# A convolution slot moved to the border between two products, and loads paced earlier, in a fused convolution and gated product

## The chip, the core and the metric

The kernel runs on one core of one Trainium2 chip. A core has engines that run beside each other: TensorE (matmuls, which write to PSUM), VectorE and ScalarE (which read PSUM and write SBUF), GpSimd and SyncE; the last two here mostly issue DMAs. In the profile they are PE (with PEld for the loading of weights), DVE, ACT, POOL and SP. The metric is the device time of one launch in microseconds (us). The kernel before takes 523.81 us, the median of three runs between 523.74 and 524.0.

## What is computed

The reference has two parts. The first is a causal convolution along the sequence, with 7 taps that each of 8 heads has for its 24 channels; the taps are a softmax of the weights. The second is a product of two projections, followed by two more products:

```python
# B, S, D = 8, 3904, 192; H, K = 8, 7; group = D // H = 24
w = softmax(weight)                                   # per head, over the 7 taps
out = np.einsum('hk,bskhg->bshg', w, x_unf)           # x_unf: x padded by 6 rows, windows of 7
x = out.reshape(B * S, D)                             # 31232 x 192
a = x @ w1                                            # 192 -> 1024
b = x @ w2
h = a * b @ w3                                        # 1024 -> 1024
return (h @ w_out).astype(np.float32)                 # 1024 -> 192
```

## The kernel before

**Tokens and rounds.** The 31232 tokens are cut in two streams of 15616 (`NS = 2`), which lie side by side: 64 of the 128 partitions belong to each. A round is 512 tokens of each stream (`CH`); there are 31 rounds (`NR`), the last of 256. Four rounds form a group (`GROUP`); there are eight groups, 0 to 7, the last of three rounds.

**First product** (`first_product`, L361, matmuls at L374). For a round and each of its eight feature tiles of 128 (0 to 7 in the text), twelve matmuls of 64 x 128 weights on 512 tokens make product a and product b of both streams. Each product fills one pair of PSUM banks. ScalarE copies a to SBUF (L380); VectorE multiplies the copy with b out of PSUM and writes the tile of `abT` (L381). Its input is `xT`, the transposed convolution, in three slices k of 128 channel rows, in a ring for four rounds (`RING`).

**Second product** (`second_product`, L388, matmuls at L400). `w3` and `w_out` are multiplied once at the start (`w3_product`, L433), so that one product from 1024 to 192 is left. For a round and one stream it takes 32 matmuls into one pair; ScalarE copies the result to `osb` (L405), and a DMA stores it (L412).

**PSUM pairs.** There are four pairs. `banks()` takes the first of a list of free ones and `drained()` puts a pair at the end of it, so all users take the pairs in rotation, in the order in which the program is written. A matmul that is to write a pair waits until the reader of its last content is done.

**Convolution** (`conv`, L262, matmuls at L278). The tokens are cut in 272 windows of 58 new tokens and 6 rows before them (64 rows). A head of a block of windows takes four 64 x 64 matmuls side by side with a banded matrix (`Aband`) as the weights' side and the block's x on the other. One head takes one pair, and VectorE (in group 0 partly ScalarE) moves it to `convo` (L295); heads 2 and 5 are moved in two pieces. Blocks 0 to 3 are small and belong to the prologue; blocks 4 to 9 have 36 windows, block 10 has 20. Block 4 is convolved in group 0 besides block 5, block 5 + p in group p.

**From the convolution back to the products.** When the last head of a block is moved, `store` (L300) writes it to DRAM (`rows`, L318 and L314), and `transposes` (L343, L347) reads it back transposed into `xT`, three DMAs to a round. Both are issued by SyncE's queue, which holds the output stores too and works strictly in order. `send(last)` (L479) issues the transposes of all rounds up to `last` whose rows are stored; after the first product of round R it is called with R + 4, since that product frees the ring for it. So a block's rows are normally needed a whole group after they are stored. The rows of block 4 are an exception: they feed rounds 4 to 7, which is group 1, right behind the group in which block 4 is convolved.

**Order of the work.** The program's order is written out by hand. In each group after the first come the first products of its rounds, then eight second products (two streams for each round, numbered 0 to 7), and between those the heads of one block, in three slots: `at` says after which second product which heads stand. The text calls the place where first products end and second products begin the border. Group 0's first products are in the prologue; its second products have six slots, three with block 4 and three with block 5.

**Loads of x.** GpSimd's queue issues them (`load_x`, L98, L112) in two halves of a block, one after each of the first two first products of the group that convolves it. What holds them back is a copy of two elements (`pace`, L528), which waits until a certain tile of `abT` is written. `zero` (L504, L506) then clears the padding rows of windows that begin a sequence.

Of the kernel before, what the change touches and what calls it, by code (L numbers as in the profile page):

```python
# [16 lines left out]
def kernel(  # L17
# [13 lines left out]
    H, K = weight.shape  # L31
    G = D // H
    DFF = moe_w1.shape[1]
    JT = DFF // 128
# [6 lines left out]
    GROUP = 4  # L41
# [9 lines left out]
    NB = len(SIZES)  # L51
# [4 lines left out]
    def tok(i):  # L56
        return (i // WB) * S + (i % WB) * ST
# [78 lines left out]
    pace = const.tile([1, 2], BF16)  # L136
# [31 lines left out]
    for p0 in (0, Q):  # L168
        nc.gpsimd.affine_select(
            out=diag[p0:p0 + Q], in_=ones[p0:p0 + Q].to_broadcast([Q, Q + PAD]),  # L170
# [3 lines left out]
    for r in range(NS):  # L174
        nc.gpsimd.dma_start(out=xb0[Q * r + PAD:Q * r + Q, 0, :],
                            in_=x_rows[r * TS:r * TS + ST, :])
# [13 lines left out]
    def warm(n, t=None):  # L190
# [16 lines left out]
        out=wall, in0=wall, in1=wmax.unsqueeze(2).to_broadcast([1, H, K]), op=ALU.subtract)  # L207
# [6 lines left out]
        out=wrow, in0=wall, in1=wsum.unsqueeze(2).to_broadcast([1, H, K]), op=ALU.mult)  # L214
# [47 lines left out]
    def conv(b, h0, nh, evict=None):  # L262
        n = SIZES[b] // 2
        if h0 == 0:
            convo_of[b] = work.tile([128, n, NP, NS, Q], BF16, tag="convo", bufs=2, name="convo")
        convo = convo_of[b]
        p, cps = banks()
        wd = nh * G

        def view(ps, r):  # L270
            return cps[ps, r, 0:n * wd].rearrange("p (w g) -> p w g", g=wd)

        for j in range(nh):
            h = h0 + j
            for c in range(2):
                xb, w0 = xb_of[b][c]
                for r in range(NS):
                    nc.tensor.matmul(  # L278
                        view(slice(Q * c, Q * c + Q), r)[:, :, j * G:(j + 1) * G],
                        band_of(h, r),  # L280
                        xb[Q * r:Q * r + Q, w0:w0 + n, h * G:(h + 1) * G],
                        start=True, stop=True)
        src = cps[:, :, 0:n * wd].rearrange("p r (w g) -> p r w g", g=wd)
        o, moves = 0, []
        for k, c0, m in segments(h0 * G, wd):
            moves.append((convo[:, :, k, :, c0:c0 + m].rearrange("p w r g -> p r w g"),
                          src[:, :, :, o:o + m]))
            o += m
        if h0 + nh == H:
            del xb_of[b]  # L290
        if evict == ():
            return p, moves
        for e, (dst, part) in enumerate(moves):
            f = evict or [nc.scalar.copy]
            f[e % len(f)](out=dst, in_=part)  # L295
        drained(p)
# [3 lines left out]
    def store(b, first=0, last=NWIN, queue=nc.sync):  # L300
        n = SIZES[b] // 2
        last = min(last, FIRST[b] + 2 * n)
        stored[0] = tok(last) if last < NWIN else TS
        convo = convo_of[b]
        for c in range(2):
            i0 = FIRST[b] + c * n
            w, end = max(0, first - i0), min(n, last - i0)
            while w < end:
                left = WB - 1 - (i0 + w) % WB
                m = min(end - w, max(1, left))  # L310
                src = convo[Q * c:Q * c + ST, w:w + m].rearrange("s w k r g -> s w (k r g)")
                j0 = tok(i0 + w)
                if left == 0:
                    queue.dma_start(out=rows[j0:j0 + LAST, :], in_=src[0:LAST, 0, :])  # L314
                else:
                    dst = rows[j0:j0 + ST * m, :].rearrange("(w s) c -> s w c", s=ST)
                    for s0, s1 in ((0, 48), (48, ST)):
                        queue.dma_start(out=dst[s0:s1], in_=src[s0:s1])  # L318
                w += m
# [36 lines left out]
    abT_of = {}  # L356
# [4 lines left out]
    def first_product(R, between=None):  # L361
        N = width(R)
        ab = work.tile([128, JT, NS, CH], BF16, tag="abT", bufs=GROUP, name="abT")
        abT_of[R] = ab
        r0 = (R * CH) % RING
        for ft in range(JT):
            pq = []
            for i in range(2):
                q, p = banks()
                pq.append((q, p))  # L370
                for k in range(NP):
                    for r in range(NS):
                        rs = slice(Q * r, Q * r + Q)
                        nc.tensor.matmul(  # L374
                            p[:, r, 0:N], wd[i][rs, k, ft * 128:(ft + 1) * 128],
                            xT[k][rs, r0:r0 + N],
                            start=(k == 0), stop=(k == NP - 1))
            (qa, pa), (qb, pb) = pq
            asb = work.tile([128, NS, CH], BF16, tag="asb", bufs=3, name="asb")
            nc.scalar.copy(out=asb[:, :, 0:N], in_=pa[:, :, 0:N])  # L380
            nc.vector.tensor_tensor(out=ab[:, ft, :, 0:N], in0=asb[:, :, 0:N],  # L381
                                    in1=pb[:, :, 0:N], op=ALU.mult)
            drained(qa)
            drained(qb)
            if between and ft in between:
                between[ft]()
# [55 lines left out]
    V, A, P = nc.vector.tensor_copy, nc.scalar.copy, nc.gpsimd.tensor_copy  # L442
# [33 lines left out]
    def need(R):  # L476
        return next(i for i in range(NWIN) if tok(i) >= (R + 1) * CH)

    def send(last):  # L479
        while sent[0] <= min(last, NR - 1) and min((sent[0] + 1) * CH, TS) <= stored[0]:  # L480
            transposes(sent[0])
            sent[0] += 1
# [21 lines left out]
    def zero(b):  # L504
        for xb, r, w in zero_rows.pop(b, []):
            nc.gpsimd.memset(xb[Q * r:Q * r + PAD, w, :], 0.0)  # L506

    def conv_heads(b, heads, f=(nc.vector.tensor_copy,), first=None):
        for j, h in enumerate(heads):
            conv(b, h, 1, (f[j % len(f)],))  # L510
        if heads[-1] == H - 1:
            store(b) if first is None else (store(b, last=first), send(NR), store(b, first))

    slots = (range(0, 3), range(3, 6), range(6, H))
    zero(4)
    for jt in range(JT):
        w3_product(jt)
# [3 lines left out]
    for p, rounds in enumerate(groups):  # L521
        b = PROLOGUE_BLOCKS + p
        order = rounds[-1:] + rounds[:-1] if rounds[-1] == NR - 1 else rounds
        for j, R in enumerate(order if p else ()):
            first_product(R)
            send(R + GROUP)
            if j < 2 and b < NB:
                P(out=pace, in_=abT_of[R][0:1, JT - 1, 1, 0:2])  # L528
                load_x(b, (j,))
        if b < NB:  # L530
            zero(b)
        at = {1: [(b, slots[0])], 3: [(b, slots[1])], 5: [(b, slots[2])]}
        if p == 0:
            at = {0: [(4, slots[0], (V, A))], 1: [(4, slots[1], (V, A))],
                  2: [(4, slots[2], (V, A), need(GROUP))], 4: at[1], 5: at[3], 6: at[5]}
        for i, (R, r) in enumerate((R, r) for R in rounds for r in range(NS)):
            second_product(R, r, R == NR - 1 and r == 1, nc.sync if p else nc.gpsimd)
            for c in at.get(i, ()) if b < NB else ():
                conv_heads(*c)
            if p == 0 and i == 2:  # L540
                send(2 * GROUP - 1)
# [31 lines left out]
```

## Time and profile before

| what | value |
|---|---|
| median of the runs | 523.81 us |
| time of the profiled execution | 523.65 us |
| its span, from first to last instruction | 521.9 us |
| TensorE busy in the span | 513.1 us (98%) |
| VectorE, ScalarE, GpSimd busy | 360.1, 322.3, 59.0 us |
| first products, L374 | 319.9 us busy, 2976 matmuls |
| second products, L400 | 166.1 us busy, 1952 matmuls |
| convolution, L278 | 16.6 us busy, 352 matmuls |
| granted clock of TensorE | 1.000 |

The profile follows one execution of the program. Its groups of instructions carry the line of the kernel, the engine, the operation and the names of the tiles. A chain of waits is followed back from the last instruction; an engine whose name stands on nearly all of the chain sets the time. Timelines give the start and the length of pieces of work in us from the start of the span, and in brackets the idle time before and what ended it. A matmul's recorded length covers its whole passage through the array, so matmuls overlap; what one costs is the distance from one start to the next. The time of a run is 1.75 us above the span of the profiled execution. The landing of SyncE's DMAs is not in the timelines, but the trace keeps every update of the semaphores that they raise.

### The profile page before, as it was taken

The page shows a single profiled execution, that of the slowest core. Times are in us where ns is not written, and L with a number is a line of the kernel's source. Part 1 is how long each engine was busy: PE and PEld are TensorE (multiplying, and loading weights), DVE is VectorE, ACT ScalarE, POOL GpSimd, SP SyncE. Part 2 cuts the span into 40 slices and gives each one's busy share as a digit, 9 for nine tenths or more (in the row PEclk, how much of TensorE's full clock was granted, in tenths as well). Part 3 has the DMA queues.
Part 4 walks back from the last instruction along what each step waited for, and adds up shares of the span by engine and source line. Part 5 has one row for each costly group of instructions (what it writes and reads, how often), then busy time and mean ns, then how long its engine had stood idle before and what let it go on. Part 6 is the DMA issues. An engine that isn't in the chain of part 4 may idle for free.

```text
span 521.9 us, 12776 instructions
## 1 busy us (share of the span) xinstructions
PE 513.1 (98%) x5452; PEld 340.3 (65%) x5452; DVE 360.1 (69%) x350; ACT 322.3 (62%) x405; POOL 59.0 (11%) x99
## 2 busy tenths in 40 slices
PE   8999899999999999999999999999999999999997
PEld 4544588545894558945588455884558855599667
DVE  6779646799537995389953899538994299912880
ACT  5877553777437774377743777437774377735762
POOL 8420522030000200003000020000200000000000
PEclk9999999999999999999999999999999999999999
DMA  9995998799656973569735696457724531024004
GB/s 127 206 155 104 141 197 253 168 188 158 142 152 162 114 104 92 156 164 124 92 98 154 159 125 88 107 150 163 99 49 120 154 97 33 17 92 152 3 1 152
DMA packets 135179, 65.39 MB, mean 125 GB/s; under 512 B 91980, under 2 KB 134318, under 8 KB 135058
## 3 DMA queue, kind: packets, MB, share of 16 engines
q1 hardware_dynamic: 95952, 44.45, 37.2%
q0 software_dynamic: 39024, 20.03, 29.3%
q8 instruction: 42, 0.69, 0.6%
q14 instruction: 15, 0.12, 0.1%
q10 hardware_dynamic: 146, 0.10, 0.1%
HBM read 33.25 MB, written 36.92 MB: 134 GB/s over the span
## 4 chain that ended last, share of the span: by engine, by line
PE 91%; DMA 3%; SPq 2%; ACT 2%; DVE 1%; issue 1%; POOL 0%; POOLq 0%; ACTq 0%
PE pairs L374 56%; PE pairs L400 31%; PE pairs L278 2%; DMA w3T<-w3rows 2%; SPq L430 2%; ACT asb L380 1%; DVE abT L381 1%; DMA xb<-in_x_dram 1%; PE pairs L436 0%; DVE convo L295 0%; PE pairs L327 0%; POOL xb L165 0%; DVE convo L445 0%; ACT xT L445 0%; SPq L347 0%
## 5 line engine op out<-in xcount | busy, mean ns | idle before, releaser
L381 DVE TENSOR_TENSOR abT<-asb,pairs 128x1024 bf16<-128x1024 bf16 (+1 forms) x248 | 298.4, 1204 | 74.2 <-ACT asb L380 37.1
L374 PE MATMUL pairs<-xT,wd 64*128 64x512 bf16 (+1 forms) x2976 | 319.9, 373 | 1.1 <-DVE convo L295 0.3
L380 ACT CAST asb<-pairs 128x1024 bf16<-128x1024 f32 (+1 forms) x248 | 247.6, 998 | 69.7 <-PE pairs L374 69.2
L374 PEld LDWEIGHTS <-wd 64*128 64x128 bf16 x2976 | 162.6, 94 | 152.9 <-issue 3.2
L400 PE MATMUL pairs<-W_sb,abT 128*128 128x192 bf16 x1952 | 166.1, 246 | 0.0
L400 PEld LDWEIGHTS <-abT 128*128 128x128 bf16 x1952 | 159.6, 98 | 9.7 <-issue 9.7
L405 ACT COPY osb<-pairs 128x384 f32<-128x384 f32 x122 | 58.2, 477 | 116.1 <-PE pairs L400 116.1
L295 DVE CAST convo<-pairs 128x864 bf16<-128x864 f32 (+6 forms) x71 | 53.0, 803 | 69.3 <-PE pairs L278 69.3
L112 POOL DMA_DIRECT2D xb<-in_x_dram x40 | 30.9, 790 | 9.0 <-issue 4.9
L528 POOL COPY pace<-abT 1x2 bf16<-1x2 bf16 x10 | 1.7, 174 | 238.7 <-DVE abT L381 238.7
L278 PE MATMUL pairs<-xb,Aband 64*64 64x432 bf16 (+3 forms) x352 | 16.6, 294 | 0.2 <-DMA xb<-in_x_dram 0.2
L278 PEld LDWEIGHTS <-Aband 64*64 64x64 bf16 x352 | 6.6, 105 | 7.1 <-issue 6.3
L412 POOL DMA_DIRECT2D out_dram<-osb x8 | 6.1, 760 | 18.5 <-ACT osb L405 18.5
L405 DVE COPY osb<-pairs 128x192 f32<-128x192 f32 x1 | 0.4, 358 | 11.1 <-PE pairs L400 11.1
L436 PE MATMUL pairs<-wo_b,w3T 128*128 128x192 bf16 x64 | 5.6, 246 | 1.9 <-DMA w3T<-w3rows 1.9
L436 PEld LDWEIGHTS <-w3T 128*128 128x128 bf16 x64 | 5.2, 98 | 2.5 <-DMA w3T<-w3rows 2.1
L295 ACT CAST convo<-pairs 128x512 bf16<-128x512 f32 (+4 forms) x11 | 6.2, 604 | 0.5 <-PE pairs L278 0.4
L438 ACT CAST W_sb<-pairs 128x192 bf16<-128x192 f32 x8 | 2.5, 318 | 4.8 <-PE pairs L436 4.8
L318 POOL DMA_DIRECT2D rows<-convo x6 | 3.5, 590 | 16.3 <-DVE convo L295 11.1
L195 PE MATMUL pairs<-zeros 128*128 128x512 bf16 x8 | 3.7, 595 | 1.3 <-DVE zeros L145 1.3
L327 PE MATMUL pairs<-identw,convo 128*128 128x128 bf16 x42 | 3.2, 219 | 1.0 <-DVE convo L445 0.6
L506 POOL MEMSET xb<- 6x192 bf16 x6 | 1.5, 249 | 21.4 <-DMA xb<-in_x_dram 21.4
(52 smaller groups left out, 42.5 us busy)
## 6 DMA issues: line engine op xcount, KB each, us to landing
out_dram<-osb SPq DMA_DIRECT2D x52, 384.0 KB
xb<-in_x_dram POOLq DMA_DIRECT2D x18, 432.0 KB, 7.3
rows<-convo SPq DMA_DIRECT2D x8, 648.0 KB
out_dram<-osb POOLq DMA_DIRECT2D x8, 384.0 KB, 5.0
w3rows<-in_moe_w_dram POOLq DMA_DIRECT2D x2, 1024.0 KB, 11.1
xb<-in_x_dram POOLq DMA_DIRECT2D x6, 240.0 KB, 6.7
xT<-rows SPq DMA_TRANSPOSE x84
rows<-convo SPq DMA_DIRECT2D x4, 324.0 KB
```

What stands on the lines that cost most here:

```text
L112: nc.gpsimd.dma_start(out=xb[Q * r:Q * r + Q, w:w + m, :], in_=x_spans(r, i, m))
L195: nc.tensor.matmul(t[:, j % 2, :], zeros[:, 0:128], zeros, start=True, stop=True)
L278: nc.tensor.matmul(view(slice(Q * c, Q * c + Q), r)[:, :, j * G:(j + 1) * G], band_of(h, r), xb[Q * r:Q * r + Q, w0:w0 + n, h * G:(h + 1) ...
L295: f[e % len(f)](out=dst, in_=part)
L374: nc.tensor.matmul(p[:, r, 0:N], wd[i][rs, k, ft * 128:(ft + 1) * 128], xT[k][rs, r0:r0 + N], start=(k == 0), stop=(k == NP - 1))
L380: nc.scalar.copy(out=asb[:, :, 0:N], in_=pa[:, :, 0:N])
L381: nc.vector.tensor_tensor(out=ab[:, ft, :, 0:N], in0=asb[:, :, 0:N], in1=pb[:, :, 0:N], op=ALU.mult)
L400: nc.tensor.matmul(ops[:, (g - g0) * D:(g - g0) * D + D], ab[:, jt, r, g * 128:(g + 1) * 128], W_sb[:, jt, :], start=(jt == 0), stop=(jt = ...
L405: f(out=osb[:, g0:g0 + per, :].rearrange("p g d -> p (g d)"), in_=ops[:, 0:per * D])
L412: queue.dma_start(out=out[t0:t0 + ng * 128, :].rearrange("(g p) d -> p g d", p=128), in_=osb)
L430: nc.sync.dma_start_transpose(out=w3T[:, gt, j:j + CH], in_=w3rows[j:j + CH, gt * 128:(gt + 1) * 128])
L436: nc.tensor.matmul(wps[:, 0, 0:D], w3T[:, gt, jt * 128:(jt + 1) * 128], wo_b[:, gt, :], start=(gt == 0), stop=(gt == JT - 1))
```

## The change

Two things are changed. First, the heads of a block are cut in slots of 2, 3 and 3 instead of 3, 3 and 2, and in groups 1 to 5 the first slot moves to the border, before the first second product; the other two stand after the second products 1 and 3. The slot after 5 is gone. In group 0 the slots stay where they are, with the new numbers of heads for block 4 and block 5. Second, the copy that paces the loads of x reads tile 3 of `abT` (the middle of a first product) instead of tile 7 (its end).

```diff
-    slots = (range(0, 3), range(3, 6), range(6, H))
+    slots = (range(0, 2), range(2, 5), range(5, H))
...
             if j < 2 and b < NB:
-                P(out=pace, in_=abT_of[R][0:1, JT - 1, 1, 0:2])
+                P(out=pace, in_=abT_of[R][0:1, JT // 2 - 1, 1, 0:2])
                 load_x(b, (j,))
         if b < NB:
             zero(b)
-        at = {1: [(b, slots[0])], 3: [(b, slots[1])], 5: [(b, slots[2])]}
+        at = {1: [(b, slots[1])], 3: [(b, slots[2])]}
         if p == 0:
             at = {0: [(4, slots[0], (V, A))], 1: [(4, slots[1], (V, A))],
-                  2: [(4, slots[2], (V, A), need(GROUP))], 4: at[1], 5: at[3], 6: at[5]}
+                  2: [(4, slots[2], (V, A), need(GROUP))],
+                  4: [(b, slots[0])], 5: [(b, slots[1])], 6: [(b, slots[2])]}
+        elif b < NB:
+            conv_heads(b, slots[0])
         for i, (R, r) in enumerate((R, r) for R in rounds for r in range(NS)):
             second_product(R, r, R == NR - 1 and r == 1, nc.sync if p else nc.gpsimd)
             for c in at.get(i, ()) if b < NB else ():
```

## The prediction

> **What bounds the kernel now.** I read the busy shares first, then the chain of waits in order of time, then single records at the places that the change touches, and the DMA queues there.
>
> ```profile
> span 521.9 us, 12776 instructions
> PE 513.1 (98%) x5452; PEld 340.3 (65%) x5452; DVE 360.1 (69%) x350; ACT 322.3 (62%) x405; POOL 59.0 (11%) x99
> ```
>
> TensorE is busy 98% of the span. The chain of waits in order of time, group 1 (rounds 4 to 7), shows how tight it is:
>
> ```profile
> 92.07 41.55 PE pairs L374 x384
> 133.62 5.39 PE pairs L400 x64
> 139.00 0.67 PE pairs L278 x12
> 139.67 5.39 PE pairs L400 x64
> 145.06 0.67 PE pairs L278 x12
> 145.73 5.39 PE pairs L400 x64
> 151.12 0.49 PE pairs L278 x8
> ```
>
> First products (L374), second products (L400) and convolution slots (L278) follow without a pause, in all groups to the seventh. So every pause that the change opens on TensorE is paid in full, and all that it can win is what lies between these pieces. Two things could open a pause: a PSUM pair that isn't drained at the border, and an xT that isn't there. The second was close already. SyncE's queue, GpSimd's queue, then VectorE and ScalarE in the stretch around the border of groups 0 and 1 (start, duration):
>
> ```profile
> 77.60 0.86 SPq L318 DMA_DIRECT2D rows<-convo  x2
> 83.29 3.77 SPq L347 DMA_TRANSPOSE xT<-rows  x3
> 97.12 12.50 SPq L347 DMA_TRANSPOSE xT<-rows  x9
> 109.72 7.16 SPq L318 DMA_DIRECT2D rows<-convo  x4
> ```
>
> ```profile
> 104.33 0.17 POOL L528 COPY pace<-abT 1x2 bf16<-1x2 bf16 x1 [10.70 <-DVE abT L381]
> 104.87 1.74 POOL L112 DMA_DIRECT2D xb<-in_x_dram  x2 [0.37 <-PE pairs L374]
> ```
>
> ```profile
> 76.48 1.06 DVE L295 CAST convo<-pairs 128x864 bf16<-128x864 f32 x1 [1.33 <-PE pairs L278]
> ```
>
> ```profile
> 76.69 0.88 ACT L295 CAST convo<-pairs 128x864 bf16<-128x864 f32 x1
> ```
>
> The nine transposes issued from 97.12 feed rounds 5, 6 and 7. Round 5 starts on TensorE at 102.37, and its third k slice is read at 102.80; the trace's semaphore updates put the landing of that slice at 102.45. So round 5 has 0.35 us to spare, the smallest margin that I found. The reader is to see what comes next: x for block 6 is issued at 104.87, after that. What such a load does to transposes stands in the packets by queue (q1 carries transposes and stores, q0 the loads of x), at 100 to 103, before the load:
>
> ```profile
> q1 hardware_dynamic: 1461, 0.36, 52.7%
> ```
>
> and at 106 to 109, just after it was issued:
>
> ```profile
> q0 software_dynamic: 801, 0.31, 99.5%
> q1 hardware_dynamic: 47, 0.01, 2.5%
> ```
>
> For 3 us the transposes all but stand still.
>
> **Part 1: the slot at the border (groups 1 to 5).** Removed: the third slot. The single records give it: last second product to first conv matmul 176 ns, two heads up to the next second product 492 ns, less the 83 ns that two second products stand apart: 0.586 us (group 5, with the short block: 0.426). Added: last first product to first conv 306 ns (the prologue has this passage six times, 306 each), two heads 492, less the 308 that this border costs now: 0.490 (0.330). Without waits a border wins 0.096 us, 0.48 us in five groups.
>
> But the pairs rotate. Head 0 takes the pair that held product a of feature tile 6 of the last round, which ScalarE drained before the border (copy ends 132.727, border 133.24). Head 1 takes product b of tile 6, which VectorE reads until 133.978, 0.738 us after the last first product started; 0.734 to 0.736 in the other borders. From VectorE's end to a waiting matmul it takes 54 ns (28.641 to 28.695, and 29.774 to 29.829). So head 1 starts at 0.79 instead of 0.306 + 0.207 = 0.513: 0.276 us of pause. The second product behind it needs ScalarE's copy of tile 7 (ends 0.782 after), and starts at about 1.07: no further wait. Per border -0.096 + 0.276 = +0.18; in group 5 the heads are shorter (0.127 apart), the pause 0.356, +0.26. Sum 4 x 0.18 + 0.26 = **+0.98 us**. Bounds: -0.48 if VectorE were done in time; if the second product had to wait for VectorE's tile 7 (ends 135.323, 2.08 after) a border would cost 2.08 + 0.05 - 0.31 - 0.59 = 1.2, so +6; the pair that it takes was read by ScalarE, so I stay at 0.98. Behind the waiting head stand only second products; VectorE's evictions of the two heads come after tile 7 and are done 4 us past the border, before the next slot (6.4 past it) wants their pairs.
>
> **Part 2: stores.** Rows of blocks 6 to 10 are issued two second products earlier, ahead of four output stores in SyncE's queue instead of two. Those rows are read a group later, and an output buffer is reused five stores later: cost 0, hidden by the whole of the next first products. In group 0 the slots become 2, 3, 3 heads instead of 3, 3, 2: the same sum on TensorE. But the first store of block 4 (77.60) now waits for three heads instead of two: VectorE takes head 5 (two pieces) and then head 7, ScalarE head 6. With conv 0.18 us earlier, VectorE's pieces run 76.30 to 77.41 (0.448 and 0.748, overlapping) and 1.06 more to 78.39. The store is issued 0.83 us later; what arrives of that at the transposes from 97.12 lies between 0 (the queue before it lands at 82 to 83 anyway) and 0.83; I take 0.4.
>
> **Part 3: the loads of x.** The pace now reads feature tile 3 of the first round instead of 7: VectorE ends that one at 99.016 in group 1, so the pace copy runs at 99.15 and the two loads are issued from 99.7, not 104.87 (the same 0.54 behind the copy). Round 5's third transpose is issued at 99.74 plus 0.4. What one costs by its place, from semaphore updates: of nine issued 0.3 to 0.7 us after a pace copy, eight landed after 4.6 to 7.95 us, median 6.1 (one, where the load itself came late, after 2.65); those issued 0.3 us or more ahead of one, after 2.5 to 4.4. Ours is issued 1.0 after. The row nearest in place and offset is round 7's in the same group (0.69 after: 7.95), the others say 6.1; I take 7.0, so it lands at 107.2, wanted at 102.80: **+4.4 us** of pause. Ends: 99.74 + 4.6 gives 1.5, 100.57 + 8.07 (the longest) gives 5.8. Round 6's slices then land by about 111, wanted at 112.7 plus the pause; round 7's later still. In groups 2 to 5 the transposes paced against are those of the next group, 30 us and more ahead of their use: 0. The border needs x for block 6 at 133.5; the load that today ends at 130.1 starts 5 us earlier and the border moves out with the pause: 0.
>
> **Sum.** 523.65 (the profiled execution) + 0.98 + 4.4 = 529.0; the median of the runs shown lies 0.16 above that execution, so I say **529.2**.
>
> **Rivals.**
> - The loads do not hold up round 5 (its packets get through ahead, as the one that landed after 2.65): only part 1 is left, with 0 to 0.5 us for the store that comes later. 523.81 + 1.0 to 1.5: 524.8 to 525.3. For it: the load's data began only 1.2 us after its issue (at 106.1). Against: eight of nine.
> - Not slower: VectorE releases head 1's pair before the border reaches it. It decides at 0.513 us after the last first product, VectorE is at 0.79; it would have to be 0.28 us faster, and round 5 unharmed too. Then -0.48: 523.3.
> - A longer pause: round 5's slice lands only after both loads (the second landed 10.1 after its pair's issue at 104.87, so 109.8): 7.0 instead of 4.4, 531.8. Or the pause costs speed after it: the first matmuls of the trace stand 0.427 us apart for 512 columns, from 7.2 us on half that; a slow stretch as long as that one (5.9 us) would add 2.9: 532. Against: the 1.9 us pause at 62.5 is followed by second products at 83 ns each, full speed. The profile shows a granted clock of 1.00 in both places, so it doesn't tell. The Trainium skill ("TensorE: Matmul & The Clock Gate", part 1) has the array fall to half its clock after an idle window of about 3.4 us, for as long again; by that page 529.2 would become about 530.9, an estimate. The full speed after 1.9 us agrees with it; no run here shows a longer pause.
>
> **How the numbers follow.** Chances: forecast (a pause of 1.5 to 5.8, so 526.3 to 530.6) 0.57; loads harmless 0.15; not slower 0.05; longer 0.23. 0.2% is 1.05 us, about what a measurement of this kernel can tell from no change. Slower: 0.57 + 0.23 + 0.06, since loads harmless lies around that line from 1.0 up: 0.86. Within: 0.09 + 0.04 = 0.13. Faster by over 0.2%: 0.01, since even the full gain of part 1 is 0.09%. The range of 8 in 10 leaves out the two cases at the low end, and reaches to the longer pause: 525.6 to 532.0.
>
> **What would show it.** Right: TensorE idle for some us at the start of round 5, near 102.6, released by the DMA of xT; five pauses of 0.28 us (0.36 in group 5) inside L278 at the borders, released by VectorE L381; loads of x issued near 99.7; no third slot. Wrong: L374 from 92 on without a gap (the loads don't matter), or second products that start over 1.1 us after the last first product (another wait at the border). What would make me wrong most easily is the share that the load's packets leave to the transposes, which I have only from neighbours.

## The result, and the profile after

The changed kernel takes 525.88 us (median of 17 executions, 524.14 to 532.81), the kernel before 523.92 (17 executions, 523.41 to 526.33). The ratio is 1.0033, with a 95% interval of 1.0017 to 1.0048: the change makes the kernel slower by about 2 us. This ratio and those below come from the fast executions alone (here without the one of 532.81 us) and are not the quotients of the medians. The forecast was 529.2, so the sign was right and the size too large by more than a factor of two.

The profiled execution of the changed kernel takes 525.22 us, 1.57 more than that of before. The page's busy line:

```profile
span 523.5 us, 12784 instructions
PE 513.0 (98%) x5452; PEld 340.0 (65%) x5452; DVE 360.6 (69%) x350; ACT 322.2 (62%) x405; POOL 59.1 (11%) x99
```

TensorE does the same work in the same busy time; the span is longer by what it stands still. Of the 1.6 us by which the spans differ, 0.54 arose in the prologue, which is the same code: the first product of group 1 starts at 92.54 instead of 92.00. From there to the end of the span it is 430.97 us, against 429.94 before: **+1.03 us**. I compare kernels by this rest below, as it leaves the prologue out.

Where the 1.03 lies, the chain of waits in order of time shows at the border of group 1 (start, duration, engine and line):

```profile
92.61 39.62 PE pairs L374 x366
132.23 0.02 issue
132.26 1.02 ACT asb L380
133.28 0.02 issue
133.30 1.23 DVE abT L381
134.53 0.04 issue
134.57 0.38 PE pairs L278 x4
134.95 5.39 PE pairs L400 x64
140.34 0.67 PE pairs L278 x12
```

Before, L374 went straight over into L400 here. Now the chain leaves TensorE, goes through ScalarE's copy and VectorE's multiplication of a feature tile, and comes back to TensorE with head 1's four matmuls (L278 x4), 0.04 us after VectorE's end. That is the wait of head 1 for VectorE's tile 6. The timeline of TensorE at group 2's border shows the same as a length:

```profile
199.21 0.86 PE L278 MATMUL pairs<-xb,Aband 64*64 64x432 bf16 x8
200.01 5.45 PE L400 MATMUL pairs<-W_sb,abT 128*128 128x192 bf16 x64
```

Two heads at 199.21, the second product at 200.01. From the single records: 306 ns from the last first product to the first conv matmul, 0.791 to 0.796 us from there to the second product (0.714 in group 5), and 472 to 477 ns from head 0 to head 1, where 207 would be free. Per border that is 0.796 + 0.306 - 0.308 - 0.586 = +0.208, in group 5 +0.286; the five make 1.1, and the rest measured 1.03.

There is no pause at round 5. L374 runs unbroken through the whole of group 1 in this execution:

```profile
92.54 41.61 PE L374 MATMUL pairs<-xT,wd 64*128 64x512 bf16 x384
```

SyncE's queue and GpSimd's queue show how near it was:

```profile
78.99 0.91 SPq L318 DMA_DIRECT2D rows<-convo  x2
84.25 3.84 SPq L347 DMA_TRANSPOSE xT<-rows  x3
96.75 14.60 SPq L347 DMA_TRANSPOSE xT<-rows  x9
111.44 7.70 SPq L318 DMA_DIRECT2D rows<-convo  x4
```

```profile
99.69 0.17 POOL L528 COPY pace<-abT 1x2 bf16<-1x2 bf16 x1 [5.52 <-DVE abT L381]
100.23 1.73 POOL L112 DMA_DIRECT2D xb<-in_x_dram  x2 [0.36 <-PE pairs L374]
```

The load of x is issued at 100.23. The single records put the issue of round 5's third transpose at 99.54, that is 0.69 us ahead of it, and the semaphore updates its landing at 102.31, 2.77 after; TensorE wants that slice at about 103.35. In the packets by queue at 100 to 102.4 the transposes (q1) still get through beside the load (q0):

```profile
q1 hardware_dynamic: 805, 0.19, 36.0%
q0 software_dynamic: 54, 0.02, 22.5%
```

Only round 6's slices met the load: they landed 6.8 to 9.2 us after their issue, but are wanted a round later, so nothing waited.

### The profile page after: what moved, and what is told of

It reads as the page before. It is cut to its first block, busy times and chain, and to the rows that moved or that the text cites. A ratio compares the mean times of both kernels' runs of the same rounds, so it can differ in the third digit from the quotient of the medians.

```text
span 523.5 us, 12784 instructions
## 1 busy us (share of the span) xinstructions
PE 513.0 (98%) x5452; PEld 340.0 (65%) x5452; DVE 360.6 (69%) x350; ACT 322.2 (62%) x405; POOL 59.1 (11%) x99
## 4 chain that ended last, share of the span: by engine, by line
PE 88%; DMA 3%; DVE 3%; ACT 2%; SPq 2%; issue 1%; POOL 0%; POOLq 0%; ACTq 0%
PE pairs L374 54%; PE pairs L400 31%; PE pairs L278 2%; DVE abT L381 2%; ACT asb L380 2%; DMA w3T<-w3rows 2%; SPq L430 2%; DMA xb<-in_x_dram 1%; PE pairs L436 0%; DVE convo L295 0%; PE pairs L327 0%; POOL xb L165 0%; SPq L347 0%; DVE convo L445 0%; ACT xT L445 0%
## 5 line engine op out<-in xcount | busy, mean ns | idle before, releaser
L381 DVE TENSOR_TENSOR abT<-asb,pairs 128x1024 bf16<-128x1024 bf16 (+1 forms) x248 | 298.4, 1204 | 94.9 <-ACT asb L380 57.8
L374 PE MATMUL pairs<-xT,wd 64*128 64x512 bf16 (+1 forms) x2976 | 320.0, 373 | 1.1 <-DVE convo L295 0.3
L374 PEld LDWEIGHTS <-wd 64*128 64x128 bf16 x2976 | 162.4, 94 | 153.1 <-issue 3.5
L400 PE MATMUL pairs<-W_sb,abT 128*128 128x192 bf16 x1952 | 165.2, 247 | 0.0
L400 PEld LDWEIGHTS <-abT 128*128 128x128 bf16 x1952 | 159.9, 98 | 6.9 <-issue 6.8
L278 PE MATMUL pairs<-xb,Aband 64*64 64x432 bf16 (+3 forms) x352 | 17.6, 295 | 2.2 <-DMA xb<-in_x_dram 1.6
L278 PEld LDWEIGHTS <-Aband 64*64 64x64 bf16 x352 | 7.1, 105 | 11.6 <-issue 10.8
```

The lines of the kernel that those rows point to most:

```text
L278: nc.tensor.matmul(view(slice(Q * c, Q * c + Q), r)[:, :, j * G:(j + 1) * G], band_of(h, r), xb[Q * r:Q * r + Q, w0:w0 + n, h * G:(h + 1) ...
L374: nc.tensor.matmul(p[:, r, 0:N], wd[i][rs, k, ft * 128:(ft + 1) * 128], xT[k][rs, r0:r0 + N], start=(k == 0), stop=(k == NP - 1))
L400: nc.tensor.matmul(ops[:, (g - g0) * D:(g - g0) * D + D], ab[:, jt, r, g * 128:(g + 1) * 128], W_sb[:, jt, :], start=(jt == 0), stop=(jt = ...
```

## The experiments

All executions scatter by more than before's first three runs let one think, and one cause is seen in the records: TensorE's granted clock falls to 0.5 for single stretches of 3.41 us. One stretch costs 1.7 us, half its length. An execution without any has a mean clock of 1.000 or 0.999 (the profiled one of e2 has 0.999 and no stretch); one stretch brings the mean to about 0.997, two to 0.993. By this measure such stretches turn up in executions of all kernels, before among them. Where it helps, medians are therefore also given for executions with a mean clock of 1.000 alone. The kernels e1 to e4 ran on one chip, e5 to e8 on another, e9 and e10 on a third, each beside before; the medians of before there were 524.75, 525.70 and 525.97. Below, "the rest" is the time from the start of group 1 to the end in the profiled execution, and the figure in brackets its distance from before's 429.94.

### e1: the slots alone

```diff
-                P(out=pace, in_=abT_of[R][0:1, JT // 2 - 1, 1, 0:2])
+                P(out=pace, in_=abT_of[R][0:1, JT - 1, 1, 0:2])
```

This line of the changed kernel is set back to tile 7.

> The new slots, with the loads of x paced as before (tile 7). Theory A (two causes: a fixed wait at five borders, and in group 1 loads of x that hold up transposes in some executions): only the borders are left, 4 x 0.21 + 0.29 = 1.1 us; the median lies 0.9 to 1.3 us above the kernel before, and the executions scatter no more than those of the kernel before. Rival B (the later first store of block 4, behind a slot of three heads in group 0, holds up round 5): as the changed kernel, some 2 us above, with executions 3 to 9 us above.

525.57 us against 524.75, ratio 1.0005 (0.9983 to 1.0027). At a mean clock of 1.000 the medians are 524.77 (7 executions) and 524.14 (13). By the medians alone a microsecond can't be told from nothing here. The profile can: the rest is 430.96 us (+1.02), with the five border waits and no other. Rival B finds no support: round 5 has no pause in the profile, and no execution is above 528.12, where before reached 528.13 on that chip.

### e2: the loads alone

```diff
-                P(out=pace, in_=abT_of[R][0:1, JT - 1, 1, 0:2])
+                P(out=pace, in_=abT_of[R][0:1, JT // 2 - 1, 1, 0:2])
```

This is before with the new pace.

> The slots of the kernel before, with the loads of x paced by half a first product. Theory A: no border costs anything; the median is 0 to 1.5 us above the kernel before, and single executions are 2 to 8 us above, with a pause at the start of round 5 or 6 where the profile catches one. Rival B: as the kernel before, within 0.3 us.

528.28 us against 524.75, ratio 1.0046 (1.0015 to 1.0076). Its executions go from 524.28 to 533.16. The profiled one has a pause, in TensorE's timeline behind the first 100 matmuls of group 1:

```profile
93.00 10.96 PE L374 MATMUL pairs<-xT,wd 64*128 64x512 bf16 x100
106.38 30.83 PE L374 MATMUL pairs<-xT,wd 64*128 64x512 bf16 x284 [2.41 <-DMA xT<-rows]
```

Its releaser is the DMA of xT. The third slice was issued 0.17 us ahead of the load and landed 5.83 later. So the mechanism of the third part of the prediction exists, with the loads alone as its cause; but the lowest three executions, 524.28, 524.31 and 525.15 at a mean clock of 0.999 to 1.000, have no room for a pause of that size. The expectation had the median 0 to 1.5 us above before, and it is 3.5 above: the loads alone cost more than the loads and the slots together. With the old slots the third transpose was issued later (7.51 us behind the start of group 1, in the changed kernel 7.00 and, in e9, 7.37), which fits; one profile of e2 does not show that it is the reason.

### e3: the late loads in group 1 only

```diff
-                P(out=pace, in_=abT_of[R][0:1, JT // 2 - 1, 1, 0:2])
+                P(out=pace, in_=abT_of[R][0:1, JT - 1 if p == 1 else JT // 2 - 1, 1, 0:2])
```

> The changed kernel, but in group 1 alone the loads of x are paced by tile 7 again. Theory A: as the slots alone, 0.9 to 1.3 us above the kernel before, without the long executions. If the long executions stay, the loads of groups 2 to 5 or the slots are behind them.

525.44 us against 524.75, ratio 1.0012 (0.9992 to 1.0031); highest 527.68, where the changed kernel reached 532.8. In the profile the rest is 431.04 (+1.10) without a pause. So the early loads of groups 2 to 5 cost nothing that can be seen, as predicted, and what the loads cost lies in group 1. Five of its twelve executions still had a lower clock (median 527.24): those stretches do not need the early loads.

### e4: the load of group 1 far ahead of round 5

```diff
-                P(out=pace, in_=abT_of[R][0:1, JT - 1, 1, 0:2])
+                P(out=pace, in_=abT_of[R][0:1, 0 if p == 1 else JT - 1, 1, 0:2])
```

This is before with the load of group 1 behind the first feature tile.

> The kernel before, but in group 1 the loads of x are paced by tile 0, so that they are issued near 96.3, ahead of round 5's transposes (97.1). Theory A: the transposes of round 5 land 4.6 to 8 us after their issue in every execution, 102 to 108, where 102.4 to 102.8 is wanted: a pause of 1 to 5 us on TensorE at the start of round 5, median 525 to 529. If the clock falls after such a pause, matmuls right behind it stand 0.43 us apart instead of 0.216, and 1 to 3 us more. Rival (loads and transposes share the engines without harm): as the kernel before.

533.1 us against 524.75 (5 executions, none below 531.64), ratio 1.0141 (1.0114 to 1.0168). TensorE's timeline:

```profile
94.05 10.53 PE L374 MATMUL pairs<-xT,wd 64*128 64x512 bf16 x96
107.75 0.61 PE L374 MATMUL pairs<-xT,wd 64*128 64x512 bf16 x2 [3.17 <-DMA xT<-rows]
109.27 31.00 PE L374 MATMUL pairs<-xT,wd 64*128 64x512 bf16 x264 [0.91 <-DMA xT<-rows]
```

With the load 1 us ahead of all three transposes each slice is late: the first landed 8.84 us after its issue, the second 8.74, the third 7.17. That is more than the 525 to 529 us expected, and three stretches of half clock have a part in it, one of them in the prologue (at 66.15) and two in a row at the pause. Windows of this trace (length, busy time of PE and its matmuls, granted clock, DMA share, GB/s):

```profile
107.00:113.80 6.80, 5.14 (x24) 0.51 0.92 138
114.00:118.00 4.00, 4.00 (x40) 1.00 0.90 139
```

### e5: the load just ahead of round 5's third transpose

```diff
-                P(out=pace, in_=abT_of[R][0:1, JT // 2 - 1, 1, 0:2])
+                P(out=pace, in_=abT_of[R][0:1, 2 if p == 1 else JT // 2 - 1, 1, 0:2])
```

This is the changed kernel with group 1's loads one feature tile (1.3 us) earlier still.

> The changed kernel, but in group 1 the loads of x are paced by tile 2 instead of 3, so that they are issued 1.3 us earlier, 6.4 us after the group's start, where round 5's third transpose is issued 7.0 to 7.5 after it. Theory A (the loads hold up whatever transpose is issued after them, and the changed kernel escapes by some tenths of a us in most executions): now every execution pauses at the start of round 5, by 2 to 5 us, and the median is 3 to 6 us above the kernel before, where the prediction had the changed kernel. Rival (the transposes get through anyway): as the changed kernel, within 1 us.

532.14 us against 525.70 (4 executions, 530.85 to 533.39), ratio 1.0127 (1.0100 to 1.0154). Now the load is 0.85 us ahead of the third transpose, the order that the prediction took for the changed kernel, and the slice lands 8.08 us after its issue:

```profile
91.90 10.97 PE L374 MATMUL pairs<-xT,wd 64*128 64x512 bf16 x100
107.26 32.51 PE L374 MATMUL pairs<-xT,wd 64*128 64x512 bf16 x284 [4.39 <-DMA xT<-rows]
```

From start to start that is a step of 4.77 us in place of 0.216, a pause of 4.55; the prediction had 4.4. The median lies 6.4 us above before, just over the 3 to 6 expected, which had no half clock in them. Behind the pause the matmuls stand 0.427 us apart for one stretch (the windows of this trace, same columns):

```profile
104.00:107.00 3.00, 0.00 (x0) 1.00 1.95 160
107.00:110.50 3.50, 3.24 (x16) 0.54 1.65 181
110.50:114.00 3.50, 3.50 (x34) 0.97 0.84 158
```

The clock is down from 107.31 to 110.73, 3.41 us, and up again after that. The sum closes: 1.03 for the borders, 4.55 for the pause and 1.7 for the half clock make 7.28; the rest measured 437.23, +7.29.

### e6 and e7: round 5's transposes taken out of the race

In group 0 the rows of block 4 that round 5 needs are stored as a piece of their own, and round 5's transposes are issued right behind it. e6 does that to the changed kernel:

```diff
-    def conv_heads(b, heads, f=(nc.vector.tensor_copy,), first=None):
+    def conv_heads(b, heads, f=(nc.vector.tensor_copy,), first=()):
...
-            store(b) if first is None else (store(b, last=first), send(NR), store(b, first))
+            for i0, i1 in zip((0,) + first, first + (NWIN,)):
+                store(b, i0, i1)
+                if first:
+                    send(NR)
...
-                  2: [(4, slots[2], (V, A), need(GROUP))],
+                  2: [(4, slots[2], (V, A), (need(GROUP), need(GROUP + 1)))],
```

> The changed kernel, with the second store of block 4 cut at the end of round 5, and round 5's transposes issued right behind it, before the rest of the block is stored (one window more in a DMA of its own). The culprit, the early load, stays; the victim is taken out of its way. Theory A: round 5's slices land some 4 us before they are wanted, no pause there; first products of group 1 to the end 1.1 us longer than in the kernel before, the five borders; no executions beyond the scatter of the kernel before. If long executions stay, they come from round 6 or from elsewhere.

e7 does the same to before.

> The same early transposes of round 5 in the kernel before. Theory A: from group 1 to the end as the kernel before, 429.9 us. If part of the scatter of the kernel before comes from its 0.35 us of margin at round 5, its long executions become fewer and the median is 0 to 0.7 us lower; if it all comes from the prologue, nothing changes.

The third transpose of round 5 is now issued 2.3 us behind the start of group 1 instead of 7.0 (e6) and 2.5 instead of 7.7 (e7), and lands more than 5 us ahead of its use, while the load of e6 stays at 7.69. SyncE's queue and TensorE in e6:

```profile
92.41 3.78 SPq L347 DMA_TRANSPOSE xT<-rows  x3
```

```profile
92.54 41.61 PE L374 MATMUL pairs<-xT,wd 64*128 64x512 bf16 x384
```

e6 takes 525.59 against 525.70, ratio 1.0007 (0.9987 to 1.0026), its rest is 430.86; e7 takes 525.29, ratio 0.9993 (0.9976 to 1.0011), its rest 429.78. So with the race gone the early loads cost nothing in this profile, and what stays of the change is the 1.08 us between these two rests: the borders. Taken alone, e7's piece of store would be a safety margin: its highest execution of 11 is 525.74, where before reached 528.36 in 23 on that chip. But the medians are not told apart, and no trace shows before itself pausing at round 5.

### e8: three heads at the border

```diff
-    slots = (range(0, 2), range(2, 5), range(5, H))
+    slots = (range(0, 3), range(3, 6), range(6, H))
...
-                P(out=pace, in_=abT_of[R][0:1, JT // 2 - 1, 1, 0:2])
+                P(out=pace, in_=abT_of[R][0:1, JT - 1, 1, 0:2])
```

This tests the rotation of PSUM pairs: with a third head, the next second product takes the pair that VectorE's tile 7 releases.

> The slots 3, 3, 2 with the first one, three heads, at the border, and the loads of x paced by tile 7. Theory A (pairs in rotation): the third head takes the pair that ScalarE reads last (free at 0.82 us after the last first product) and the second product behind it the pair that VectorE reads last (free at 2.13), so it starts at 2.13 instead of 1.1: per border 2.13 - 0.31 - 0.77 = 1.06 us, 1.3 in group 5, together 5.5 us above the kernel before, with two pauses at each border, 0.28 us inside the slot and 0.8 us behind it. Rival (the pause in the slot comes from another thing than the pair, as the loading of weights or the waits for x): the second product follows the third head by 0.285 us, and the whole is 1 to 1.5 us above.

529.74 us against 525.70 (4 executions), ratio 1.0092 (1.0062 to 1.0122). TensorE's timeline at group 2's border:

```profile
200.05 1.04 PE L278 MATMUL pairs<-xb,Aband 64*64 64x432 bf16 x12
201.83 5.36 PE L400 MATMUL pairs<-W_sb,abT 128*128 128x192 bf16 x63 [0.74 <-DVE abT L381]
```

The second product waits for VectorE's L381, and starts some 2.1 us after the last first product, which is the bound that the prediction named for that case (2.08 plus 0.05). The rest is 435.76, +5.8, of which 0.64 is a pause at round 5 that this profile had even with the late load: its third transpose was issued 8.63 us behind the start of group 1, the latest of those with the late load, and landed as usual after 2.78. So a late transpose alone can open this pause, without a load. What is left for the five borders is 5.2 us, of 5.5 expected.

### e9: the changed kernel again

The changed kernel without any edit, for another look at the race.

> The changed kernel once more, to see its executions beside the kernel before on one chip, with the mean granted clock of each. Theory A: its executions at full clock lie 1.1 us and, where round 5 pauses, up to 5 us above those of the kernel before; more of its executions than of the kernel before have two slow windows of 3.4 us (mean clock near 0.993), as the early loads alone have, since a pause of some us at round 5 brings one. Rival: nothing but the five borders, 1.1 us, at every clock.

527.35 us against 525.97, ratio 1.0047 (1.0019 to 1.0074). Its rest is 433.09 us (+3.15), and this time the profiled execution has the pause:

```profile
92.42 10.97 PE L374 MATMUL pairs<-xT,wd 64*128 64x512 bf16 x100
105.34 30.82 PE L374 MATMUL pairs<-xT,wd 64*128 64x512 bf16 x284 [1.96 <-DMA xT<-rows]
136.10 0.86 PE L278 MATMUL pairs<-xb,Aband 64*64 64x432 bf16 x8
```

The third transpose was issued at 99.79, the load at 100.11: 0.32 us between them where the first profile had 0.69. The slice landed 5.51 us after its issue instead of 2.77, a pause of 2.12; with 1.03 for the borders that is the whole of the 3.15. At 101 to 104 the load takes the engines:

```profile
q0 software_dynamic: 641, 0.25, 79.5%
q1 hardware_dynamic: 537, 0.13, 20.1%
```

So one program has executions with and without the pause, and what separates the two that were traced is 0.37 us in the offset of two queues. That the offset decides it is what e5 and e6 bear out, which move one of the two queues. One of the twelve executions had a mean clock of 0.993, none of before's 23: too few to judge what was expected of such executions.

### e10: a slot behind the last second product

This edit starts from e7. It seeks a place for the third slot where it saves a passage between tile shapes as the border does, without the wait: behind the last second product, ahead of the next group's first product.

```diff
-        at = {1: [(b, slots[0])], 3: [(b, slots[1])], 5: [(b, slots[2])]}
+        at = {1: [(b, slots[0])], 3: [(b, slots[1])], 7: [(b, slots[2])]}
...
-                  2: [(4, slots[2], (V, A), (need(GROUP), need(GROUP + 1)))], 4: at[1], 5: at[3], 6: at[5]}
+                  2: [(4, slots[2], (V, A), (need(GROUP), need(GROUP + 1)))], 4: at[1], 5: at[3], 6: at[7]}
```

> The kernel before with round 5's early transposes, and with the third slot (two heads) moved to the other border, behind the last second product and ahead of the next group's first product. Theory A: there the pairs are free (ScalarE has copied them 0.8 us after the last matmul's start, and VectorE is idle), so the passage that two borders share is won: 0.586 - 0.490 = 0.096 us in each of five groups, less 0 to 0.1 where the second tile of the first product waits for VectorE's eviction of the second head: from the start of group 1 to the end 429.3 to 429.9 us, against 429.9, with no pause inside the slot.

524.87 us against 525.97, ratio 0.9995 (0.9976 to 1.0013); the rest is 430.02, against 429.78 in e7. No gain, and just outside the 429.3 to 429.9 expected: the passage saves its 0.09 us in a group, but the second feature tile of the next group now waits 0.12 us for VectorE's eviction (in four of the five groups; with the short block it does not wait). The border's mistake returns on the other side, smaller. None of these kernels is shown to beat before.

## Why the prediction was right and wrong

**Part 1, the slot at the border: right.** Predicted +0.98 us, from five waits for VectorE's tile 6. Measured +1.1 by the five borders, +1.03 by the rest, and 0.92 to 1.10 in e1, e3 and e6, which have these slots and no pause. Head 1's step of 483 ns (0.276 of wait beyond 207) is 472 to 477, and VectorE's tile 6 ends 0.740 us after the last first product (0.738 predicted). The term that came out larger is the passage: I had put head 1 at 0.79 and the second product at 1.07 us behind the last first product, and it starts at 1.10. That the pairs rotate as read is shown by e8, where one head more turns the wait to VectorE's tile 7, to the predicted place.

**Part 2, the later store: the step was right, what arrives of it was not.** The first store of block 4 was issued 0.85 us later against the start of group 1 (0.83 predicted). But of that I had let 0.4 us reach round 5's transposes, and they came earlier: the third was issued 7.00 us behind the start of group 1, before 7.74. Over the profiles it was 7.00 to 7.50 in the five with the new slots and the stores in one piece (the changed kernel twice, e1, e3, e5), and 7.51 to 8.63 in the four with the old slots (before, e2, e4, e8). The queue swallowed the delay, as the lower bound had it (0), and more. Why the new slots come out ahead I have not settled: part of it is that TensorE's start of group 1 moved (92.00 to 92.54) while the queue did not move with it (third transpose at 99.74 before, 99.54 after), but the two profiles of the changed kernel alone differ by 0.37 us (7.00 and 7.37).

**Part 3, the loads: right in the mechanism, wrong in the offset.** This is the step that failed. It read "issued 1.0 after" the pace copy: round 5's third transpose at 99.74 + 0.4 against a copy at 99.15. Measured in the first profile, the transpose was issued at 99.54 and the copy ran at 99.69, so the transpose was 0.15 ahead of the copy, 0.69 ahead of the load itself. The load came as forecast (7.69 us behind the start of group 1, forecast 7.70); the transpose came 1.14 us earlier (7.00 behind it, forecast 8.14), as the 0.4 us of part 2 did not arrive and another 0.74 was gained. With that the 4.4 us of pause fell away in this execution. The same transpose in four executions:

| kernel | third transpose issued, against the load | landed after its issue | pause |
|---|---|---|---|
| changed, first profile | 0.69 us ahead | 2.77 us | none |
| e9, changed again | 0.32 ahead | 5.51 | 2.12 |
| e2 | 0.17 ahead | 5.83 | 2.57 |
| e5 | 0.85 behind | 8.08 | 4.55 |

I had computed 4.4 us for the last line's order and charged it to every execution. That e5 paused 4.55 is in part luck: its slice took 8.08 us to land instead of the 7.0 that I took, but was issued 0.90 us earlier against the start of group 1. The changed kernel lies in the first two lines, with no pause in one and 2.12 in the other.

The prediction's own rows held the answer, but it measured them from the pace copy, and the load stands 0.45 to 0.97 us behind that. Measured from the load, the nine transposes lie between 0.63 ahead of it and 0.15 behind. The one at 0.63 ahead is the one that landed after 2.65 us, of which the prediction only says that its load came late; it is the nearest row to the first profile (0.69 ahead, 2.77). The other eight lie from 0.22 ahead to 0.15 behind, and took 4.6 to 7.95.

The two terms of the offset come from different queues: the load stands at 7.68 or 7.69 us behind the start of group 1 in each of the four profiles with tile 3 there (the changed kernel twice, e2, e6), bound to TensorE; the transposes stand in SyncE's queue behind stores, and came 7.00 to 7.51 behind that start in the three of these that keep the stores in one piece. A margin of 0.2 to 0.7 us against a wander of 0.5 is no fixed outcome, and I treated both queues as if one profile fixed them.

**The rivals.** "Loads harmless" (524.8 to 525.3, chance 0.15) is what the first profile shows, and its 1.0 us for the borders is right. That this execution, 525.22, lies inside the range is partly luck, as 0.54 of its 1.57 us come from the prologue. The median lies 0.6 above that range; executions that pause, as e9's did, are the likely reason. "A longer pause, and speed lost after it" (0.23) is seen in a trace only where the experiments made the pause longer. The longest executions of the changed kernel (532.81, in e9 531.51 and 532.53) may be such cases, but have no trace. "Not slower" would have needed VectorE to be 0.28 us faster at the border; it was not.

In e5 a pause of 4.55 us was followed by 3.41 us at half the clock. The Trainium skill ("TensorE: Matmul & The Clock Gate", part 1) has the array fall to half its clock after an idle window of about 3.4 us, for as long again, with windows that run on freely; e5 and the stretches of 3.41 us agree. But the idle time need not fill a window, other than the page has it, and its length alone does not decide: in e4 a step of 2.63 us at the wait for w3T in the prologue (at 62.2) was followed by such a stretch at 66.15, in e2 a step of 2.74 us at the same place was not. The clock records of each trace lie on a grid of 3.41 us. In e4 one window of it (62.73 to 66.15) held 2.07 us of idle time; in e2 a boundary at 64.20 cut the step, so that two windows held 1.41 and 1.08. In e10 a window with 2.00 us was followed by a stretch, in before one with 1.88 was not, and in e7 1.61 us near the start of the program were enough, so no threshold is shown.

**Sum by the measured terms.** 1.03 us for the borders, and a pause of 0 to some 2 us where a trace shows it, with or without a stretch of half clock: the median of +1.96 lies between. The longest executions leave room for more: 532.81, at two stretches by its mean clock, is 8.9 us above before's median, and the borders and two stretches make 4.4 of that. How many of the changed kernel's executions paused stays open, as only the profiled ones have a trace: two, of which one did. That the pauses make up the part of the median above 1.03 is thus an inference from e2, e3 and e9, not a count.

## What to carry to other kernels

A price read from neighbouring rows ("a transpose behind a load lands after 6 us") holds only with the offset at which they stood. When the offset of two queues is a few tenths of a microsecond, and one is bound to the compute engine and the other to earlier DMAs, forecast a chance for each execution and not one outcome; then either give the transfer a margin (an earlier store, as in e6) or leave the load alone. Work that is moved to a border between two kinds of matmuls should be followed through the rotation of PSUM pairs to the engine that drains the pair it gets: that reading alone gave the cost of this move to about a tenth of a microsecond, and for the variant with three heads to about a tenth for each border.

## What had not been expected

- A load need not be ahead of a transpose to hold it up: issued 0.32 us behind it, it still doubled the time to its landing (5.51 us, against 2.77 where it was issued 0.69 us behind). In e5 the second transpose, 0.45 us ahead of the load, lies between them with 4.40. The prediction's rows show it too, once they are measured from the load.
- Half-clock stretches are 3.41 us long wherever they were seen (66.15 to 69.56 in e4, 107.31 to 110.73 in e5, 10.14 to 13.55 in e7, 64.87 to 68.29 in e10, and two in a row in e4 from 107.11 to 113.93), and each costs 1.7 us. They make a kernel's times fall into steps, of the kernel before too: on one chip 7 of its 23 executions had a mean clock of 1.000 (median 523.72) and 14 one of 0.997 or less (526.01). A change of 1 us is below these steps, and only the profiles could measure it.
- Of the first three runs of before, none differed from another by more than 0.26 us; over 75 more executions on the three chips of the experiments the same kernel went from 523.09 to 528.36.
